# One core, attention and a mixture of experts: the last selection in another order, half of a comparison on GpSimd and ScalarE, the first block of tokens copied alone

## The chip, the cores and the metric

The kernel runs on one NeuronCore of a Trainium2 chip. Its engines work side by side and each takes its own instructions in the order of the program: TensorE (PE, with the weight loads as PEld), VectorE (DVE), ScalarE (ACT), GpSimd (POOL) and SyncE (SP), which issues most DMAs. An instruction waits on semaphores for what other engines owe it, and everything behind it on its engine waits too. The metric is the device time of one execution in microseconds, the median of several.

## The reference

Causal attention for 8 batches, 12 heads, 448 positions and 64 values per head, then a mixture of 8 experts over the 3584 tokens of 768 values. Each token goes to one expert, the one with the largest gate logit; an expert keeps at most 80 tokens, those with the largest gate weight. All other rows of the result are zero.

```python
scores = scale * np.matmul(q, k.transpose(0, 1, 3, 2))
attn = softmax(np.where(mask, -1e9, scores))
x = (attn @ v).transpose(0, 2, 1, 3).reshape(N, D)
logits = x @ w_gate
expert_idx = np.argmax(logits, axis=1)
gate_w = softmax(logits)[np.arange(N), expert_idx]
for e in range(E):
    tok_idx = np.where(expert_idx == e)[0]
    if len(tok_idx) > capacity:
        keep = np.argpartition(-gate_w[tok_idx], capacity)[:capacity]
        tok_idx = tok_idx[keep]
    h = np.maximum(x[tok_idx] @ w1[e], 0.0)
    out[tok_idx] = gate_w[tok_idx, None] * (h @ w2[e])
```

(The softmax is written short here.)

## The kernel before, in words

**Attention.** The batches follow each other. Heads go in pairs; for each pair the scores, the masked softmax, the transposes of the probabilities and the products with v are laid out by hand over eight slots. Queries and keys are split into two float16 parts (GpSimd and VectorE subtract, L387 and L395). The rows that attention gives go to a buffer in memory, xs.

**Selection.** After each batch its tokens are gated, and a table with the 80 best tokens of each expert so far is merged with those of the new batch. `gate` (L623 on) makes the logits, subtracts the largest (gsh, L641), marks the chosen expert (goh, L648 and L659) and makes the weights (ggw, gow). `select_groups` then writes the one-hot rows and the weight, cut into three bfloat16 parts, to mv (L703 to L716). Two transposes (selt, L731) and copies on ScalarE (ex, L734) turn one-hots and weights into rows. From these come rl and lt (L761, L767), which compare the tokens of the batch with the table; cp and ro, the new ranks of the table's tokens (L774, L779); rn and less (L745, L748), which compare the tokens of the batch with each other in four parts; gt, own and rank, their ranks (L813 to L830). `place` (L783) compares ro with the slot numbers and gives rm, one-hot for the table's tokens, in two halves of four experts each; rr (L849) is the same for the new tokens. The products of rm and rr with the table and mv give the new table tn (L859, L862).

For the first seven batches all this lies under the next batch's attention. After the last batch nothing is left to hide it. There the order is written out by hand in the string `TAIL`: every name is a step, issued in this order on all engines. `r0w` to `r7w` turn the eight blocks of attention's rows on TensorE, `r0e` to `r7e` take them to SBUF on the engine that `ROW_ENGINES` names, and divide by the softmax's sums: "v" does it on VectorE, "a" in six multiplications on ScalarE (L605), "p" copies on ScalarE (L607) and scales on GpSimd (L619, step `r0m` to `r7m`); then a DMA to xs follows. `hold` issues a copy of one column on GpSimd (L721) that depends on the gating, so what stands behind it on GpSimd waits for VectorE. "*2" issues two products without use that keep TensorE busy (L1108).

**Experts.** `finish` (L915) makes the indices of the chosen tokens and their weights. `gather` fetches an expert's 80 tokens from xs with an indirect DMA (L1197), which waits for all of the DMAs to xs. `inputs` (L1202) transposes them (xtp) and splits them into float16 parts h and l, or for blocks of weights that are used whole, in float32, copies them as w (xw). Weights are split too: ScalarE casts them to wh (L1180), VectorE makes the remainder wl (L1165). Expert 0 begins with the three blocks of w1 that are used whole, so its first product (hp, L1231) needs xw alone. In this part only TensorE's order is written by hand; on the other engines a scheduler has set it.

Of the kernel before, what the change touches and what calls it, by code (L numbers as in the profile page):

```python
# [7 lines left out]
F32 = mybir.dt.float32  # L8
F32R = mybir.dt.float32r
F16 = mybir.dt.float16  # L10
BF16 = mybir.dt.bfloat16
I32 = mybir.dt.int32
AF = mybir.ActivationFunctionType
ALU = mybir.AluOpType
# [3 lines left out]
P = 128  # L18
# [23 lines left out]

TAIL = """
u ta ya tb yb v0 td yd tc yc v1 vy guard invert last_rows w gp0 wy close piece gp1 gs
r0w r0e r1w lp r1e r1m r2w r2e rest rest r3w r3e lg logit shifted chosen rest rest r4w r4e r5w *2
sums one_hot wsum one_zero wmore columns r0t r0c *2 weight weighted parts hold r1t r1c rl r3m r4m r5e r5m r6w r6e r6m
lt c3w c3l cp c2w r7w r7e r7m ro c2l c1w gt3 *1 c0w c1l gt2 *1 c0l *1 gt1 places *1 earlier gt0 places_more own *3 rank rr tn tab *17
"""
ROW_ENGINES = "vpappppp"


@with_exitstack
def attention_then_moe(
# [12 lines left out]
    nc = tc.nc  # L66
    B, _, NP, S = qT.shape
    N, D = out.shape
    E = wg.shape[2]
# [3 lines left out]
    NT = (S + P - 1) // P  # L73
    NC1 = D // P
    NC2 = F // P
    LAST = S - (NT - 1) * P
    CAP = max(0, min(int(capacity), N))
# [8 lines left out]
    spool = sel_stack.enter_context(tc.tile_pool(name="sel", bufs=2, side="right"))  # L86
    ps_m = ctx.enter_context(tc.tile_pool(name="ps_m", bufs=2, space=PSUM))
# [30 lines left out]
    SL = max(2, min(P, CAP))  # L118
    NSL = (CAP + SL - 1) // SL
# [12 lines left out]
    for r in range(2):  # L132
        t = akeep.tile([P, OFF_L + NT * P], F32, name=f"prob{r}")
# [7 lines left out]
    for r in range(2):  # L141
        t = akeep.tile([P, NT, PH * P], F32, name=f"vt{r}")
# [41 lines left out]
    wmore = [wearly]  # L184
# [37 lines left out]
    lg = keep.tile([P, NT, H * E], F32, name="lg")  # L222
# [468 lines left out]
    def select_groups(bt):  # L691

        b = bt.b
        last = b == B - 1
        sm = lambda name, shape, dt=F32: spool.tile(shape, dt, name=name, tag=name, bufs=1)
# [23 lines left out]
        def hold():  # L719

            nc.gpsimd.tensor_copy(sm("held", [P, 1]), bt.rest[:, 0, 0:1])  # L721

        def expert_rows(i):
            got = []
# [55 lines left out]
                bt.moves.append((table[s][0], ro, sn))  # L780
            return [weights, less, counts, ranks]

        def place(ro, sn, s, rm=None):  # L783

            n = min(SL, CAP - s * SL)
            halves = [(0, E // 2), (E // 2, E)]
            if rm is not None:
                halves.pop(0)
            elif NSL == 1:
                halves.pop()  # L790
            if rm is None:
                rm = spool.tile([SL, E, SL], BF16, name="rm", tag="rm", bufs=1 if NSL == 1 else 2)
            for e0, e1 in halves:
                nc.vector.tensor_tensor(
                    out=rm[0:sn, e0:e1, 0:n], in0=ro[0:sn, e0:e1].unsqueeze(2).to_broadcast([sn, e1 - e0, n]),
                    in1=slots_e[0:sn, s, e0:e1, 0:n], op=ALU.is_equal)
            return rm
# [10 lines left out]
        def later_part(t):  # L808

            if t == NT - 1:  # L810
                bt.gt = ps_m.tile([P, NT, E], F32, name="gt", tag="misc")
            for u in range(t + 1):
                nc.tensor.matmul(bt.gt[:, u, :], bt.less[t][:, u * P:(u + 1) * P], bt.oh3[:, t, 0, :],  # L813
                                 start=(t == NT - 1 and u == 0), stop=(t == u), skip_group_check=True)
# [16 lines left out]
            bt.new = []  # L831

        def places():
            if NSL == 1:
                bt.places = [place(ro, so, 0) for tab, ro, so in bt.moves]

        def places_more():
            if NSL == 1:
                for rm, (tab, ro, so) in zip(bt.places, bt.moves):
                    place(ro, so, 0, rm)  # L840

        def move(s):
# [43 lines left out]
            if not last and NSL == 1:  # L886
# [9 lines left out]
        moves = [f for s in range(NSL) for f in move(s)]  # L896
        steps = {"columns": columns, "parts": parts, "r0t": r0[0], "r0c": r0[1], "r1t": r1[0], "r1c": r1[1],
                 "places": places, "places_more": places_more, "earlier": earlier, "own": own, "rank": rank}
        steps.update({"hold": hold, **{f"gt{t}": lambda t=t: later_part(t) for t in range(NT)}} if last else {"gt": later})
        for t in range(NT):  # L900
            steps[f"c{t}w"], steps[f"c{t}l"] = cmp[NT - 1 - t]
        if tabs:
# [36 lines left out]
    for b in range(B):  # L939
        bt = Batch()  # L940
# [7 lines left out]
    n = len(pairs)  # L948
# [33 lines left out]
    with tc.manual_schedule():  # L982
# [14 lines left out]
            out=nowhere, out_offset=None, in_=w2.rearrange("e p c (g d) -> (e p c g) d", d=DH)[0:N, :],  # L997
# [10 lines left out]
        deferred, parts = [], []  # L1008
        for i, pr in enumerate(pairs):
            bt = pr.bt  # L1010
# [7 lines left out]
            h = i // PH  # L1018
# [12 lines left out]
            for k in range(SLOTS):  # L1031
# [37 lines left out]
        rest = [f for k in sorted(plan) for f in plan.pop(k)]  # L1069
# [66 lines left out]
    ps = ctx.enter_context(tc.tile_pool(name="ps", bufs=2, space=PSUM, reuse_waits="tile"))  # L1136
# [4 lines left out]
    def whole(e, which, c):  # L1141

        if e >= E - 2:
            return e == E - 1 and which == 2 and c >= NC2 - 1
        return c >= NC2 - 2 if which == 2 else c >= (NC1 // 2 if e == 0 else NC1 - 1)

    SW, SX = 32.0, 8.0
# [3 lines left out]
    PER = NC1 if NC1 * SL <= 512 else NC1 // 2  # L1151
# [50 lines left out]
    def inputs(u):  # L1202

        h = ffn.tile([P, NC1, SL], F16, name="xh", tag="xh")
        l = ffn.tile([P, NC1, SL], F16, name="xl", tag="xl")
        nw = sum(whole(u.e, 1, c) for c in range(NC1))
        w = ffn.tile([P, NC1 // 2, SL], F32, name="xw", tag="xw", bufs=1)
        per = NC1 // 2 if u.e == 0 else PER
        for c0 in reversed(range(0, NC1, per)):
            tp = ps_m.tile([P, per, SL], F32, name="xtp", tag="misc", padded_shape=[P, PER, SL])  # L1210
            for c in range(per):
                nc.tensor.transpose(tp[:, c, :], u.xg[:, (c0 + c) * P:(c0 + c + 1) * P], ident[0:SL, 0:SL])
            part = slice(c0, c0 + per)
            if nw and c0 + per == NC1:
                nc.scalar.activation(w[:, NC1 // 2 - nw:], tp[:, per - nw:], AF.Copy, scale=SX * SW)
            nc.scalar.activation(h[:, part], tp, AF.Copy, scale=SX)
            u.xl = nc.vector.scalar_tensor_tensor(out=l[:, part], in0=tp, scalar=SX, in1=h[:, part], op0=ALU.mult,
                                                  op1=ALU.subtract)
        u.x = h, l, w

    def product(u, a, which, x, n, outs, per, blocks=None, side=None):
# [117 lines left out]
    for s in range(NSL):  # L1339
# [4 lines left out]
        for e in range(E):  # L1344
            u = Unit()
# [9 lines left out]
        with tc.manual_schedule(engines={mybir.EngineType.PE}):  # L1355
            for e in range(E + 1):
                if e < E:
                    u = units[e]
# [77 lines left out]
```

## Time and profile before

| | us |
|---|---|
| three runs, median | 467.88 (467.48 to 468.62) |
| the profiled execution | 467.61 |
| its span | 465.7 |
| attention | to about 333 |
| last selection, to the first expert product | to 351.2 |
| experts, to the last product | to about 459 |

A row of the timeline gives the start from the span's beginning, the duration, the engine, the line, the operation, what it writes and reads with its size (partitions x elements), and in brackets how long the engine stood idle before it and what ended that. Rows that begin with a line are groups, with their count, busy time and mean in ns, or with the shortest, middle and longest duration. A window's row gives each engine's busy time, and the granted TensorE clock (PEclk) as a share of full speed.

### The profile page before, as it was taken

The page shows a single profiled execution, that of the slowest core. Times are in us where ns is not written, and L with a number is a line of the kernel's source. Part 1 is how long each engine was busy: PE and PEld are TensorE (multiplying, and loading weights), DVE is VectorE, ACT ScalarE, POOL GpSimd, SP SyncE. Part 2 cuts the span into 40 slices and gives each one's busy share as a digit, 9 for nine tenths or more (in the row PEclk, how much of TensorE's full clock was granted, in tenths as well). Part 3 has the DMA queues.
Part 4 walks back from the last instruction along what each step waited for, and adds up shares of the span by engine and source line. Part 5 has one row for each costly group of instructions (what it writes and reads, how often), then busy time and mean ns, then how long its engine had stood idle before and what let it go on. Part 6 is the DMA issues. An engine that isn't in the chain of part 4 may idle for free.

```text
span 465.7 us, 14169 instructions
## 1 busy us (share of the span) xinstructions
PE 441.2 (95%) x4973; PEld 346.3 (74%) x4973; DVE 414.5 (89%) x1286; ACT 392.3 (84%) x1077; POOL 309.1 (66%) x382
## 2 busy tenths in 40 slices
PE   4998999999999999999999999999989999999994
PEld 1676666866777786677777767776558999999993
DVE  6888889988998999899899989989589999999792
ACT  6997989878988997898889789888587998988791
POOL 7999999988987987898798789760153133310001
PEclk9999999999999999999999999999999999999999
DMA  8658899989769578966957987439948999999931
GB/s 217 182 158 236 230 304 275 271 242 306 206 209 297 171 232 253 270 184 211 298 163 223 279 243 220 161 129 344 410 157 274 397 391 391 398 425 423 423 132 44
DMA packets 42998, 120.84 MB, mean 260 GB/s; under 512 B 6146, under 2 KB 23810, under 8 KB 39472
## 3 DMA queue, kind: packets, MB, share of 16 engines
q1 hardware_dynamic: 41712, 116.21, 76.8%
q0 software_dynamic: 1056, 3.51, 2.4%
q8 instruction: 39, 0.64, 0.6%
q10 hardware_dynamic: 160, 0.23, 0.2%
q14 instruction: 31, 0.25, 0.2%
HBM read 96.36 MB, written 23.99 MB: 258 GB/s over the span
## 4 chain that ended last, share of the span: by engine, by line
PE 75%; DVE 9%; POOL 5%; DMA 4%; issue 3%; ACT 2%; SPq 1%; POOLq 0%; DVEq 0%; ACTq 0%
PE xp L495 15%; PE tp L465 15%; PE sp L423 6%; PE sp L424 5%; PE rt L592 4%; PE hp L1231 3%; PE op L1231 3%; PE op L1239 3%; PE sp L433 3%; PE gp L545 3%; PE hp L1246 3%; PE hp L1245 3%; PE hp L1243 2%; DMA qk<-k_t 2%; DVE wl L1165 2%
## 5 line engine op out<-in xcount | busy, mean ns | idle before, releaser
L448 ACT ACTIVATE prob<-ns,nb 128x128 f32<-128x128 f32 (+3 forms) x336 | 177.1, 529 | 23.0 <-DVE nb L445 20.6
L445 DVE CUSTOM_DVE_ANT_0 ns<-sp,mask 128x384 f32<-128x384 f32 (+2 forms) x288 | 116.2, 413 | 20.2 <-PE sp L424 16.5
L465 PE MATMUL tp<-ident,prob 128*128 128x128 f32 x768 | 118.4, 277 | 1.1 <-ACT prob L448 0.9
L477 ACT COPY PT<-tp 128x512 f32<-128x512 f32 x182 | 104.1, 573 | 17.8 <-PE sp L423 8.4
L395 POOL TENSOR_TENSOR qk<-qk,qk 128x448 f16<-128x448 f32 x92 | 95.8, 1063 | 13.1 <-DVE qk L387 7.4
L465 PEld LDWEIGHTS tp<-ident,prob 128*128 128x128 f32 x768 | 89.8, 142 | 12.1 <-ACT PT L477 2.5
L1165 DVE SCALAR_TENSOR_TENSOR wl<-wraw,wh 128x768 f16<-128x768 f32 (+1 forms) x91 | 92.5, 1081 | 3.2 <-ACT wh L1180 3.2
L495 PE MATMUL xp<-PT,vt 128*64 128x448 f32 (+3 forms) x768 | 91.1, 380 | 0.0
L495 PEld LDWEIGHTS xp<-PT,vt 128*64 128x64 f32 x768 | 53.8, 137 | 42.7 <-issue 22.7
L423 PE MATMUL sp<-qk 128*128 128x384 f16 (+2 forms) x288 | 75.9, 279 | 8.2 <-ACT qk L355 5.2
L1180 ACT ACTIVATE wh<-wraw 128x768 f16<-128x768 f32 (+1 forms) x91 | 79.0, 931 | 3.6 <-PE hp L1246 1.8
L424 PE MATMUL sp<-qk 128*128 128x384 f16 (+2 forms) x288 | 78.3, 278 | 1.3 <-DVE qk L349 0.8
L448 ACT ACTIVATION_READ_ACCUMULATOR prob<-ns,nb 128x1 f32 x336 | 64.0, 190 | 0.0
L1332 POOL DMA_INDIRECT out<-yo,idx x8 | 14.7, 1832 | 70.8 <-ACT yo L1329 66.6
L390 POOL TENSOR_TENSOR qk<-qk,qk 64x448 f16<-64x448 f32 x46 | 54.8, 1190 | 3.4
L391 POOL TENSOR_TENSOR qk<-qk,qk 64x448 f16<-64x448 f32 x46 | 51.0, 1109 | 3.2
L423 PEld LDWEIGHTS <-qk 128*128 128x128 f16 x288 | 28.5, 99 | 17.3 <-issue 8.0
L387 DVE CAST qk<-qk 128x896 f16<-128x896 f32 x46 | 40.4, 879 | 0.1
L384 POOL CAST qk<-qk 64x896 f16<-64x896 f32 x40 | 37.4, 935 | 4.4 <-PE sp L436 3.2
L1246 PEld LDWEIGHTS <-wl 128*128 128x128 f16 x362 | 36.1, 100 | 0.9 <-DVE wl L1165 0.7
L1243 PEld LDWEIGHTS <-wh 128*128 128x128 f16 x362 | 36.4, 101 | 0.0
L1245 PEld LDWEIGHTS <-wh 128*128 128x128 f16 x362 | 36.2, 100 | 0.0
(192 smaller groups left out, 927.7 us busy)
## 6 DMA issues: line engine op xcount, KB each, us to landing
wraw<-w SPq DMA_DIRECT2D x27, 1536.0 KB, 15.7
qk<-k_t SPq DMA_DIRECT2D x92, 224.0 KB, 5.5
out<-mask_l SPq DMA_DIRECT2D x56, 192.0 KB, 4.6
qk<-q_t SPq DMA_DIRECT2D x23, 448.0 KB, 4.2
vt<-v_t SPq DMA_DIRECT2D x24, 384.0 KB, 5.7
xs<-xr SPq DMA_DIRECT2D x42, 192.0 KB, 2.9
wraw<-w SPq DMA_DIRECT2D x24, 256.0 KB, 5.9
vt<-v_t SPq DMA_DIRECT2D x24, 64.0 KB, 5.3
```

What stands on the lines that cost most here:

```text
L390: nc.gpsimd.tensor_tensor(out=qa[hi, i], in0=qf[lo, i], in1=qa[lo, i], op=ALU.subtract)
L391: nc.gpsimd.tensor_tensor(out=qb[lo, i], in0=qf[hi, i], in1=qb[hi, i], op=ALU.subtract)
L395: nc.gpsimd.tensor_tensor(out=k_lo[j][:, i], in0=kf[j][:, i], in1=k_hi[j][:, i], op=ALU.subtract)
L423: nc.tensor.matmul(sp[:, 0:w], qx[:, p, t * P:w], kx[:, p, 0:w], start=True, stop=False)
L424: nc.tensor.matmul(sp[:, 0:w], qx[:, p, t * P:w], lx[:, p, 0:w], start=False, stop=True)
L445: pr.masked = nc.vector.tensor_tensor_reduce(out=ns[:, 0:w], in0=sp[:, 0:w], in1=m, scale=-1.0 / 8.0, scalar=HUGE, op0=ALU.add, op1=ALU.mi ...
L448: nc.scalar.activation(pr.P[:, off:off + w], ns[:, 0:w], AF.Exp, bias=nb, scale=-1.0, accum_out=total)
L465: nc.tensor.transpose(pr.tp[:, i], pr.P[:, off:off + P], ident)
L477: copy(dst, src)
L495: state["pe"] = nc.tensor.matmul(xp[rows, 0:w], st["vt"][:, c, p * P + j * DH:p * P + (j + 1) * DH], pr.PT[:, j, n0:n0 + w], start=(c == 0 ...
L1165: return nc.vector.scalar_tensor_tensor(out=l, in0=src, scalar=SW, in1=h, op0=ALU.mult, op1=ALU.subtract)
L1180: nc.scalar.activation(h, src, AF.Copy, scale=SW)
```

## The change

Four things are different, all of them after attention.

1. `TAIL` is reordered. r2 is no longer scaled on ScalarE but on GpSimd, r7 no longer on GpSimd but on ScalarE (`ROW_ENGINES`); the scalings r2m, r3m and r4m stand further ahead, and the turns r6w and r7w too. The product rl stands ahead of the second transposed block, and the counts of keep-warm products differ.
2. The second half of `place` in the last selection is no longer an `is_equal` on VectorE. `apart` takes the difference of ro and the slot number on GpSimd and squares it; `joined` gives relu(1 - d*d) on ScalarE, which is one where they are equal and zero otherwise.
3. The first half stays on VectorE, where it stood (`places`).
4. `inputs` of expert 0 transposes and copies the first float32 block alone, then the two others, then the float16 blocks. For all experts, blocks that are used whole are no longer also split into h and l.

```diff
-r0w r0e r1w lp r1e r1m r2w r2e rest rest r3w r3e lg logit shifted chosen rest rest r4w r4e r5w *2
-sums one_hot wsum one_zero wmore columns r0t r0c *2 weight weighted parts hold r1t r1c rl r3m r4m r5e r5m r6w r6e r6m
-lt c3w c3l cp c2w r7w r7e r7m ro c2l c1w gt3 *1 c0w c1l gt2 *1 c0l *1 gt1 places *1 earlier gt0 places_more own *3 rank rr tn tab *17
+r0w r0e r1w lp r1e r1m r2w r2e rest rest r2m r3w r3e lg logit shifted chosen rest rest r4w r4e r3m r5w r5e *3
+sums one_hot wsum one_zero wmore columns r6w *2 r0t r0c r7w r6e *1 weight weighted parts r4m hold *1 rl r1t r1c lt *2 c3w r5m r6m c3l cp c2w
+ro places_more c2l c1w r7e moved *2 gt3 *1 c0w c1l gt2 *1 c0l gt1 places *1 earlier gt0 own *5 rank rr tn tab *20
-ROW_ENGINES = "vpappppp"
+ROW_ENGINES = "vppppppa"
...
+            bt.one = sm("one", [P, 1])
+            nc.gpsimd.memset(bt.one, 1.0)
...
+        def apart(ro, so):
+            d = sm("apart", [SL, E // 2, SL], BF16)
+            half = d[0:so, :, 0:CAP]
+            bt.apart.append((half, so))
+            nc.gpsimd.tensor_tensor(out=half, in0=ro[0:so, E // 2:E].unsqueeze(2).to_broadcast([so, E // 2, CAP]),
+                                    in1=slots_e[0:so, 0, E // 2:E, 0:CAP], op=ALU.subtract)
+            nc.gpsimd.tensor_tensor(out=half, in0=half, in1=half, op=ALU.mult)
+            return spool.tile([SL, E, SL], BF16, name="rm", tag="rm", bufs=1)
+
+        def joined():
+            for rm, (half, so) in zip(bt.places, bt.apart):
+                nc.scalar.activation(rm[0:so, E // 2:E, 0:CAP], half, AF.Relu, bias=bt.one[0:so], scale=-1.0)
...
-        per = NC1 // 2 if u.e == 0 else PER
-        for c0 in reversed(range(0, NC1, per)):
-            tp = ps_m.tile([P, per, SL], F32, name="xtp", tag="misc", padded_shape=[P, PER, SL])
+        parts = [(0, NC1)] if u.e else [(NC1 // 2, NC1 // 2 + 1), (NC1 // 2 + 1, NC1), (0, NC1 // 2)]
+        for i, (c0, c1) in enumerate(parts):
...
+            split = [c for c in range(c0, c1) if not whole(u.e, 1, c)]
+            m = len(split)
+            if m < n:
+                nc.scalar.activation(w[:, c0 + m - NC1 // 2:c1 - NC1 // 2], tp[:, m:], AF.Copy, scale=SX * SW)
+            if m:
+                nc.scalar.activation(h[:, c0:c0 + m], tp[:, 0:m], AF.Copy, scale=SX)
```

What this makes of the engines' order is shown at three places; line numbers behind the diff's places are higher in the changed kernel (the cast of weights, L1180, is L1201 there).

ScalarE, from the first row copy of the last selection to the first copies of expert 0's tokens, before (xrl are attention's rows, tab and row the table, wh the cast weights):

```order
L607 COPY xrl<-rt 128x384
L605 ACTIVATE xrl<-rt,sums 128x64 x6
L873 CAST tab_0_678<-tn 80x40
L607 COPY xrl<-rt 64x384
L646 ACTIVATE gex<-gsh 128x32
...
L734 COPY ex<-selt 24x512 x2
L607 COPY xrl<-rt 128x384 x2
L607 COPY xrl<-rt 64x384
L1180 ACTIVATE wh<-wraw 128x1024 x8
L1215 ACTIVATE xw<-xtp 128x240
L1216 ACTIVATE xh<-xtp 128x240 x2
```

The same place in the changed kernel:

```order
L607 COPY xrl<-rt 128x384 x2
L894 CAST tab_0_678<-tn 80x40
L607 COPY xrl<-rt 64x384
L646 ACTIVATE gex<-gsh 128x32
...
L736 COPY ex<-selt 24x512
L605 ACTIVATE xrl<-rt,rql 64x64 x6
L853 ACTIVATE rm<-apart,one 80x320
L1201 ACTIVATE wh<-wraw 128x1024 x8
L1241 ACTIVATE xw<-xtp 128x80
L1241 ACTIVATE xw<-xtp 128x160
L1243 ACTIVATE xh<-xtp 128x240
```

The six multiplications have moved from r2 to r7, the Relu (L853) has come in ahead of the eight casts of weights, and the copy to xw is in two parts.

GpSimd, from the first row scaling to the first gather, before (mv gets the columns of the batch's tokens):

```order
L619 TENSOR_TENSOR xrl<-xrl,sums 128x384
L703 TENSOR_TENSOR mv<-goh,tbase 128x4x8
L705 TENSOR_TENSOR mv<-goh,pnum 128x4x8
L721 COPY held<-grest 128x1
L619 TENSOR_TENSOR xrl<-xrl,rql 64x384
L619 TENSOR_TENSOR xrl<-xrl,sums 128x384 x3
```

And in the changed kernel:

```order
L619 TENSOR_TENSOR xrl<-xrl,sums 128x384 x2
L619 TENSOR_TENSOR xrl<-xrl,rql 64x384
L703 TENSOR_TENSOR mv<-goh,tbase 128x4x8
L705 TENSOR_TENSOR mv<-goh,pnum 128x4x8
L619 TENSOR_TENSOR xrl<-xrl,sums 128x384
L721 COPY held<-grest 128x1
L723 MEMSET one 128x1
L619 TENSOR_TENSOR xrl<-xrl,sums 128x384 x2
L846 TENSOR_TENSOR apart<-ro_6399,slots_e 80x320
L848 TENSOR_TENSOR apart<-apart 80x320
```

Three scalings now stand ahead of "held" where one stood, and the two operations of `apart` follow the last scaling.

VectorE, the last comparisons before the gather, in the changed kernel; before, a second row "rm<-ro" of 80x320 stood between rank and own:

```order
L750 SCALAR_TENSOR_TENSOR less_6324,parts<-rn,ggw,before 128x128
L796 TENSOR_TENSOR rm<-ro_6399,slots_e 80x320
L822 TENSOR_TENSOR parts<-parts,lower_6377 128x4
L823 TENSOR_TENSOR rank<-number_after,parts 128x4
L827 TENSOR_TENSOR own<-gt,goh 128x32
L829 TENSOR_REDUCE larger<-own 128x4
```

One row of VectorE is gone there, and the others stand as before.

More of the change, by code (lines that the diff above doesn't have):

```diff
@@ L781, in table_chunk, with place @@
             return [weights, less, counts, ranks]
-        def place(ro, sn, s, rm=None):
+        def place(ro, sn, s, rm=None, half=1):
             n = min(SL, CAP - s * SL)
@@ L787, in place @@
             if rm is not None:
-                halves.pop(0)
+                halves = halves[half:half + 1]
             elif NSL == 1:
@@ L833, in places @@
         def places():
-            if NSL == 1:
+            if last and NSL == 1:
+                for rm, (tab, ro, so) in zip(bt.places, bt.moves):
+                    place(ro, so, 0, rm, 0)
+            elif NSL == 1:
                 bt.places = [place(ro, so, 0) for tab, ro, so in bt.moves]
+        def apart(ro, so):
[9 more added lines that the diff above has]
+                nc.scalar.activation(rm[0:so, E // 2:E, 0:CAP], half, AF.Relu, bias=bt.one[0:so], scale=-1.0)
         def places_more():
-            if NSL == 1:
+            if last and NSL == 1:
+                bt.apart = []
+                bt.places = [apart(ro, so) for tab, ro, so in bt.moves]
+            elif NSL == 1:
                 for rm, (tab, ro, so) in zip(bt.places, bt.moves):
@@ L898, in select_groups @@
                  "places": places, "places_more": places_more, "earlier": earlier, "own": own, "rank": rank}
-        steps.update({"hold": hold, **{f"gt{t}": lambda t=t: later_part(t) for t in range(NT)}} if last else {"gt": later})
+        steps.update({"hold": hold, "moved": joined if NSL == 1 else lambda: None, **{f"gt{t}": lambda t=t: later_part(t) for t in range(NT)}} if last else {"gt": later})
         for t in range(NT):
@@ L1205, in inputs @@
         l = ffn.tile([P, NC1, SL], F16, name="xl", tag="xl")
-        nw = sum(whole(u.e, 1, c) for c in range(NC1))
         w = ffn.tile([P, NC1 // 2, SL], F32, name="xw", tag="xw", bufs=1)
-        per = NC1 // 2 if u.e == 0 else PER
-        for c0 in reversed(range(0, NC1, per)):
-            tp = ps_m.tile([P, per, SL], F32, name="xtp", tag="misc", padded_shape=[P, PER, SL])
[L1211 to L1218, printed above, removed]
+        parts = [(0, NC1)] if u.e else [(NC1 // 2, NC1 // 2 + 1), (NC1 // 2 + 1, NC1), (0, NC1 // 2)]
+        for i, (c0, c1) in enumerate(parts):
+            n = c1 - c0
+            if i == 0 and len(parts) > 1:
+                tp = ps.tile([P, n, SL], F32, name="xtp", tag="o", padded_shape=[P, PER, SL])
+            else:
+                tp = ps_m.tile([P, n, SL], F32, name="xtp", tag="misc", padded_shape=[P, PER, SL])
+            for c in range(n):
+                nc.tensor.transpose(tp[:, c, :], u.xg[:, (c0 + c) * P:(c0 + c + 1) * P], ident[0:SL, 0:SL])
+            split = [c for c in range(c0, c1) if not whole(u.e, 1, c)]
+            m = len(split)
+            assert split == list(range(c0, c0 + m))
+            if m < n:
+                nc.scalar.activation(w[:, c0 + m - NC1 // 2:c1 - NC1 // 2], tp[:, m:], AF.Copy, scale=SX * SW)
+            if m:
+                nc.scalar.activation(h[:, c0:c0 + m], tp[:, 0:m], AF.Copy, scale=SX)
+                u.xl = nc.vector.scalar_tensor_tensor(out=l[:, c0:c0 + m], in0=tp[:, 0:m], scalar=SX, in1=h[:, c0:c0 + m],
+                                                      op0=ALU.mult, op1=ALU.subtract)
         u.x = h, l, w
```

## Prediction

> **What bounds the kernel now.** I read the page's chain first, then a table of three stretches (the end of the selection, the expert layers, the end).
>
> ```profile
> PE 75%; DVE 9%; POOL 5%; DMA 4%; issue 3%; ACT 2%; SPq 1%; POOLq 0%; DVEq 0%; ACTq 0%
> core 0: us, PE busy (x) PEld busy (x) DVE busy (x) ACT busy (x) POOL busy (x), PEclk, DMA share, GB/s
> 335.00:351.20 16.20, 12.83 (x116) 8.05 (x114) 13.60 (x52) 13.46 (x28) 9.07 (x12) 1.00 0.53 195
> 351.20:455.00 103.80, 103.67 (x1933) 103.52 (x1934) 100.17 (x126) 90.27 (x148) 21.85 (x12) 1.00 0.92 363
> ```
>
> From 351.2 to 455.0 us TensorE is busy 103.67 of 103.80 us: whatever moves the first expert product moves the end by about as much. All of the change that can matter lies in the 16 us before, where TensorE waits. What released that first product stands in the chain of waits in order of time, and ScalarE's timeline shows it whole:
>
> ```profile
> 345.39 0.50 DVE rr L849
> 350.14 0.64 PE L1212 MATMUL xtp<-ident,xg 80*128 80x80 f32 x6 [0.65 <-DMA xg<-xs,idx]
> 342.70 1.05 ACT L1180 ACTIVATE wh<-wraw 128x1024 f16<-128x1024 f32 x1
> 344.13 6.74 ACT L1180 ACTIVATE wh<-wraw 128x1024 f16<-128x1024 f32 x7 [0.38 <-DMA xs<-xrl]
> 350.78 0.34 ACT L1215 ACTIVATE xw<-xtp 128x240 f32<-128x240 f32 x1
> 351.18 0.34 PE L1231 MATMUL hp<-xw,wraw 128*128 128x80 f32 x1 [0.40 <-ACT xw L1215]
> ```
>
> Two paths meet at xw. One is the selection on VectorE, the index, the gather and the transposes of the tokens, whose first bank is ready about half way through its 0.64 us, near 350.5. The other is ScalarE, which takes instructions in order and has eight casts of weights (wh) ahead of xw: they hold it until 350.78. The casts already end last, by 0.2 to 0.3 us. So a selection that finishes sooner buys nothing unless the casts also start sooner.
>
> **The change, step 1: row copies sooner on GpSimd.** Before, GpSimd stands idle while VectorE works out the gating; the copy "held" (L721) keeps the scalings of rows behind it.
>
> ```profile
> 336.02 0.83 POOL L619 TENSOR_TENSOR xrl<-xrl,sums 128x384 f32<-128x384 f32 x1 [2.32 <-ACT xrl L607]
> 338.49 0.26 POOL L703 TENSOR_TENSOR mv<-goh,tbase 128x32 bf16<-128x32 f32 x1 [1.64 <-DVE goh L669]
> 338.72 0.23 POOL L705 TENSOR_TENSOR mv<-goh,pnum 128x32 bf16<-128x32 f32 x1
> 339.84 0.82 POOL L619 TENSOR_TENSOR xrl<-xrl,rql 64x384 f32<-64x384 f32 x1
> 336.11 1.34 ACT L605 ACTIVATE xrl<-rt,sums 128x64 f32<-128x64 f32 x6 [0.17 <-PE rt L592]
> 337.38 0.49 ACT L607 COPY xrl<-rt 64x384 f32<-64x384 f32 x1
> 337.24 0.19 DVE L641 TENSOR_TENSOR gsh<-logit,gmx 128x32 f32<-128x32 f32 x1
> 337.47 0.19 DVE L648 SCALAR_TENSOR_TENSOR goh<-gsh,dec 128x32 f32<-128x32 f32 x1
> 339.10 0.18 DVE L713 CAST mv<-gow 128x32 bf16<-128x32 f32 x1
> 339.64 0.19 DVE L716 TENSOR_TENSOR mv<-grest,mv 128x32 bf16<-128x32 f32 x1
> ```
>
> After, the scalings of r2 and r3 follow r1 at once and r4 stands ahead of "held". What GpSimd does beside VectorE's small operations is to be seen in earlier batches (all executions of L648, then one of them with its neighbour on GpSimd, then two casts' spread):
>
> ```profile
> L648 DVE SCALAR_TENSOR_TENSOR goh<-gsh,dec x8: 191/679/851, 65.7 to 337.5; 128x32 f32<-128x32 f32 x8
> 65.44 1.04 POOL L390 TENSOR_TENSOR qk<-qk,qk 64x448 f16<-64x448 f32 x1
> 65.68 0.85 DVE L648 SCALAR_TENSOR_TENSOR goh<-gsh,dec 128x32 f32<-128x32 f32 x1
> L387 DVE CAST qk<-qk x46: 602/623/2770, 12.5 to 302.3; 128x896 f16<-128x896 f32 x46
> ```
>
> L648 takes 0.19 us alone, and in this very stretch, but 0.68 to 0.85 beside a GpSimd operation: it ends 0.05 us after GpSimd does (66.53 against 66.48). I take that price. r2 runs from 336.85 to 337.67 (0.82, as r1's row), so gsh ends at 337.72 in place of 337.43; r3 runs to 338.49, so goh ends at 338.54 in place of 337.66: **+0.88 us**. r3's copy on ScalarE (L607, 337.38 before) is early enough, since r2 now takes one such copy of 0.49 us there, not the six multiplications of 1.34. With all of it 0.88 later, L705 ends at 339.83 and r4 holds GpSimd until 340.65. The cast L713 would start at 339.98; like L387, whose spread shows that casts wait too, it then ends at 340.70 in place of 339.28: **+1.42 in all**. Were casts free, only the operation with two inputs behind it would wait, and the sum here would be 1.20; that is the lower bound. I take 1.42, as L387 is a cast of the same two types.
>
> The Trainium skill, page "SBUF — State Buffer", section on its two separate sides, says that VectorE and GpSimd share one pair of SBUF ports under an exclusive lock: an operation of VectorE with two SBUF inputs or in a two-port mode waits for the whole GpSimd instruction. By that rule step 1 costs 1.42; if the engines only shared bandwidth, nearly nothing (rival B). The rows of L648 side with the rule.
>
> **Step 2: rl ahead of the second transposed block.**
>
> ```profile
> 338.72 0.40 PE L731 MATMUL selt<-identb,oh 128*128 128x128 bf16 x4
> 339.15 0.57 ACT L734 COPY ex<-selt 24x512 bf16<-24x512 bf16 x1 [0.50 <-PE selt L731]
> 339.98 0.38 PE L731 MATMUL selt<-identb,mv 128*128 128x128 bf16 x4 [0.49 <-POOL held L721]
> 340.20 0.31 PE L761 MATMUL rl<-row,ex 128*128 128x80 bf16 x4
> 340.55 0.30 DVE L767 TENSOR_SCALAR_CACHE_REDUCE lt<-rl,ggw 128x80 bf16<-128x80 f32 x1 [0.71 <-PE rl L761]
> 341.03 0.38 PE L745 MATMUL rn<-ex 128*128 128x512 bf16 x1 [0.17 <-ACT ex L734]
> 341.44 0.75 DVE L748 SCALAR_TENSOR_TENSOR less<-rn,ggw,before 128x512 bf16<-128x512 f32 x1
> 342.12 0.22 DVE L779 TENSOR_SCALAR ro<-cp,pnum 80x8 f16<-80x8 f32 x1
> ```
>
> VectorE idles 0.71 us for rl, which stood behind the second selt; now rl comes first. But the first "less" needs rn, and rn needs the second selt, which needs mv: 341.44 is 1.61 us after mv ends (339.83), by way of selt, ex and rn, and none of that gets shorter. Lt has its 0.9 us of slack filled either way. So the swap is worth nothing, and "less" and ro follow mv: ro ends at 342.34 + 1.42 = 343.76. The extra keep-warm products stand where TensorE waits; before the gather they now number 20 at 0.2 us, 0.1 us at most ever in the way.
>
> **Step 3: half of the comparison on GpSimd and ScalarE.**
>
> ```profile
> 343.47 0.08 DVE L748 DVE_READ_ACCUMULATOR less<-rn,ggw,before 128x1 f32 x1
> 343.00 0.82 POOL L619 TENSOR_TENSOR xrl<-xrl,rql 64x384 f32<-64x384 f32 x1
> 343.47 0.70 DVE L794 TENSOR_TENSOR rm<-ro,slots_e 80x320 bf16<-80x320 f16 x1
> 344.36 0.48 DVE L794 TENSOR_TENSOR rm<-ro,slots_e 80x320 bf16<-80x320 f16 x1
> L395 POOL TENSOR_TENSOR qk<-qk,qk 128x448 f16<-128x448 f32 x92 | 95.8, 1063 | 13.1 <-DVE qk L387 7.4 <-POOL qk L391 3.7
> L1263 ACT ACTIVATE hh<-hp 128x320 f16<-128x320 f32 x9 | 3.7, 425 | 0.0
> ```
>
> VectorE loses the second L794, 0.40 us of its path. In its place GpSimd runs two operations of 80x320 on 16-bit data, which no row shows. L619 (384 columns, 0.82) and L703 (32 columns, 0.26) put 320 columns on a line at 0.72; L395 (1.06 for 448, writing 16 bits) gives 0.76 by share and 1.06 as an upper end. I take 0.75 each. Beginning 0.10 after ro: 343.86 to 344.61, and 344.65 to 345.40. The Relu on ScalarE is like L1263 (0.43 us, the next one 0.35 after its start): it starts at 345.48, and **the eight casts now stand behind it**, so they start at 345.83, not 342.70. Seven of them took ScalarE from 344.13 to 350.78, 0.95 each; eight take 7.60. ScalarE reaches xw at **353.43**.
>
> VectorE's side has meanwhile come to: last "less" 343.55 + 1.42 = 344.97, rm held by GpSimd to 345.74 (L794 ends 0.34 after it: 344.17 against 343.82), rr 0.82 later at 346.56, which is 1.17 later than before; tokens at 350.14 + 1.17 = 351.31, transposed by 351.95. The casts end 1.5 us after that, so they set the time.
>
> **Step 4: the first float32 block alone.**
>
> ```profile
> 357.27 0.24 ACT L1215 ACTIVATE xw<-xtp 128x80 f32<-128x80 f32 x1 [2.70 <-PE xtp L1212]
> ```
>
> The first copy takes 0.24, as this one of 80 columns does, rather than 0.34 us: hp starts at 353.43 + 0.24 + 0.05 = **353.72, against 351.18: +2.54**. The narrower copies of the other experts (480 to 400 columns, about 0.08 us each on VectorE and ScalarE) are off the path while TensorE is full; with the few tenths that TensorE waited in the expert layers I give back 0.2. Bounds of this: 0 to 0.7.
>
> **Sum.** The profiled execution took 467.61 us, its span 465.7 us, the median of the three runs is 467.88; the 0.27 between them are less than the bounds and are not added. 467.61 + 2.54 - 0.2 = 469.95, say **469.9 us**. From the unknown costs: step 1 lower by 0.22, step 3 higher by 0.62 (two at 1.06), give-back up to 0.7: 469.2 to 470.6.
>
> **Rivals.** *B, no waiting for GpSimd.* Mv stays at 339.83. Rl waits for the first copy to ex (339.72) and for TensorE's row turn and keep-warm ahead of it, an estimated 339.98 in place of 340.20, so the second selt, behind it, comes 0.16 late and ro ends at 342.50. The casts still stand behind GpSimd and Relu: 2.07 us later at 344.57, xw at 352.17, hp at 352.44, +1.26, with the give-back 468.7. For it: "own" and other reads of PSUM never show waits; against it: L648. *C, not slower: the expert layers take the delay up.* Weight loads and VectorE (100.17 of 103.80) are nearly as full as TensorE; if one of them set the end, hp could start up to 2.5 us later for nothing, and the result is 467.6. It decides from the point at which TensorE has gaps worth 1.4 us in that stretch; its row leaves 0.13. *D, worse:* GpSimd's operations near 1.06, and its three row scalings each waiting on VectorE in turn (another 0.5): 471.0. *E, the change does what it says:* only if the casts began by 342.6 could the gather (0.40 sooner) set the time, hp 350.6, 467.0; ro itself ends at 342.34 before, so two GpSimd operations do not fit.
>
> **How the numbers follow.** The forecast (casts late by steps 1 and 3) 0.66, B 0.18, C 0.06, D 0.08, E 0.02. The range that leaves out only C and E and takes in the bounds is 468.3 to 471.3. A measurement of this kernel tells 0.3%, 1.4 us, from no change. The forecast and D are above that, a sixth of B too; the rest of B and most of C are within; so slower 0.75, same 0.22, and 0.03 for faster, out of C and E, for a saving that I don't see.
>
> **What would show it.** Right: wh starts near 345.8, directly behind Relu; xw waits for ScalarE, not for xtp; L641 and L648 at 0.4 to 1.0 us; TensorE idle 1 to 2 us between xtp and hp. Step 1 wrong: L648 at 0.19. Step 3 wrong: GpSimd's two operations under 0.5 us. All of it is wrong if xw starts directly behind the transposes.

## The result, and the profile after

| | before | after |
|---|---|---|
| median | 467.81 us | 474.69 us (473.87 to 476.37) |
| ratio after / before | | 1.0149 (95% interval 1.0136 to 1.0163) |
| the profiled execution | 467.61 us | 475.72 us |
| its span | 465.7 us | 473.5 us |
| mean granted TensorE clock | 0.999 | 0.981 |

The change makes the kernel 6.9 us slower. Slower was forecast, by 2.1 us; 474.69 lies above the upper end of the forecast range, 471.3.

The page of the profile after shows in one row where to look. PEclk is the granted clock in 40 slices of 11.8 us; the chain's share of TensorE has grown from 75% to 84%.

```profile
PEclk9999999999999999999999999999995999999998
...
PE 84%; DVE 7%; ACT 5%; issue 2%; DMA 1%; POOL 0%; POOLq 0%; SPq 0%; DVEq 0%; ACTq 0%
```

The table of stretches of the changed kernel places it: the selection, the 13.6 us behind the first expert product, and the rest.

```profile
core 0: us, PE busy (x) PEld busy (x) DVE busy (x) ACT busy (x) POOL busy (x), PEclk, DMA share, GB/s
335.00:353.65 18.65, 14.92 (x128) 9.06 (x126) 14.59 (x51) 13.92 (x29) 11.61 (x16) 1.00 0.46 154
353.65:367.22 13.57, 13.57 (x91) 13.57 (x92) 7.56 (x9) 4.55 (x9) 1.22 (x2) 0.50 0.85 295
367.22:459.00 91.78, 91.78 (x1737) 91.76 (x1735) 88.41 (x112) 82.25 (x133) 11.63 (x9) 1.00 0.92 364
```

TensorE is "busy" in the whole of the middle stretch, at a granted clock of 0.50: 91 products, where the 13.57 us behind the first expert product before hold 254:

```profile
351.18:364.75 13.57, 13.57 (x254) 13.57 (x254) 13.14 (x17) 10.78 (x18) 2.58 (x3) 1.00 0.97 318
```

Busy time alone doesn't show it; the column PEclk does.

ScalarE's and TensorE's timelines, after (two fences, one for each engine):

```profile
334.71 0.53 ACT L550 COPY gs<-gp 96x448 f32<-96x448 f32 x1 [2.01 <-PE gp L545]
345.34 0.56 ACT L853 ACTIVATE rm<-apart,one 80x320 bf16<-80x320 bf16 x1 [1.79 <-POOL apart L848]
345.81 7.67 ACT L1201 ACTIVATE wh<-wraw 128x1024 f16<-128x1024 f32 x8
353.38 0.40 ACT L1241 ACTIVATE xw<-xtp 128x80 f32<-128x80 f32 x2
```

```profile
351.22 0.63 PE L1236 MATMUL xtp<-ident,xg 80*128 80x80 f32 x6
353.65 10.53 PE L1258 MATMUL hp<-xw,wraw 128*128 128x80 f32 x48 [1.79 <-ACT xw L1241]
363.97 1.01 PE L1236 MATMUL xtp<-ident,xg 80*128 80x80 f32 x6
```

The forecast chain is there, row by row: the Relu, eight casts behind it, xw at 353.38 (353.43 forecast), the first expert product at 353.65 (353.72). What is new is the length of that product's row: the same 48 product passes that took 5.58 us now take 10.53. Before, the copy of the gate's products, gs, and that row stood so (again one fence for each engine):

```profile
334.62 0.53 ACT L550 COPY gs<-gp 96x448 f32<-96x448 f32 x1 [2.02 <-PE gp L545]
```

```profile
351.18 5.58 PE L1231 MATMUL hp<-xw,wraw 128*128 128x80 f32 x48 [0.40 <-ACT xw L1215]
```

Attention does not end at the same moment in every execution, so from here on times of the selection are counted from the start of gs (334.71 after, 334.62 before), and those of the expert layers from the first expert product. With the starts of xtp rows in TensorE's timeline as marks:

| stretch | before | after | difference |
|---|---|---|---|
| gs to the first expert product | 16.56 | 18.94 | +2.38 |
| from there to the transposes for expert 1 | 5.42 | 10.32 | +4.90 |
| to those for expert 2 | 11.64 | 13.16 | +1.52 |
| to those for expert 7 | 67.62 | 67.33 | -0.29 |
| to TensorE's last product | 23.87 | 23.07 | -0.80 |

They add up to 7.71 us of the 7.8 by which the span grew. The first row was forecast (2.54). The next two, 6.42 us, hold the stretch at half clock. The last two are a gain, of 1.1 us.

### The profile page after: what moved, and what is told of

It reads as the page before. It is cut to its first block, busy times and chain, and to the rows that moved or that the text cites. A ratio compares the mean times of both kernels' runs of the same rounds, so it can differ in the third digit from the quotient of the medians.

```text
span 473.5 us, 14192 instructions
## 1 busy us (share of the span) xinstructions
PE 448.1 (95%) x4984; PEld 353.2 (75%) x4984; DVE 415.2 (88%) x1284; ACT 393.1 (83%) x1078; POOL 301.2 (64%) x385
## 4 chain that ended last, share of the span: by engine, by line
PE 84%; DVE 7%; ACT 5%; issue 2%; DMA 1%; POOL 0%; POOLq 0%; SPq 0%; DVEq 0%; ACTq 0%
PE xp L495 17%; PE tp L465 16%; PE sp L423 7%; PE sp L424 6%; PE hp L1258 4%; PE rt L592 4%; PE op L1266 4%; PE op L1258 3%; PE gp L545 3%; PE sp L433 3%; PE hp L1272 3%; PE hp L1273 3%; PE hp L1270 3%; DVE ns L445 2%; PE op L1268 2%
## 5 line engine op out<-in xcount | busy, mean ns | idle before, releaser
L395 POOL TENSOR_TENSOR qk<-qk,qk 128x448 f16<-128x448 f32 x92 | 97.1, 1077 | 13.6 <-DVE qk L387 8.0
L1201 ACT ACTIVATE wh<-wraw 128x768 f16<-128x768 f32 (+1 forms) x91 | 79.1, 930 | 4.8 <-PE hp L1273 2.1
L1359 POOL DMA_INDIRECT out<-yo,idx x8 | 9.4, 1175 | 74.3 <-ACT yo L1356 70.3
L387 DVE CAST qk<-qk 128x896 f16<-128x896 f32 x46 | 40.7, 885 | 1.3 <-DMA qk<-k_t 1.3
L1270 PEld LDWEIGHTS <-wh 128*128 128x128 f16 x362 | 37.0, 102 | 0.0
L1272 PEld LDWEIGHTS <-wh 128*128 128x128 f16 x362 | 36.8, 102 | 0.0
```

The costliest lines, as they stand in the source:

```text
L395: nc.gpsimd.tensor_tensor(out=k_lo[j][:, i], in0=kf[j][:, i], in1=k_hi[j][:, i], op=ALU.subtract)
L1201: nc.scalar.activation(h, src, AF.Copy, scale=SW)
L1270: nc.tensor.matmul(o, wh[:, ws], ah[:, c, :], start=(x == 0 and i % per == 0), stop=False, skip_group_check=True)
```

## The experiments

The kernel before ran beside each group of four: 468.16, 467.26 and 467.44 us. What happened at TensorE's clock, and whether 2.4 us were the casts' alone, had to be separated. The first four kernels: fill the idle time; shorten ScalarE's queue; take the comparison back; and delay xw in the kernel before, without any of the change.

**fill.**

```diff
                         inputs(u)
+                        wp = ps.tile([P, S], F32, name="wq", tag="o")
+                        for _ in range(9):
+                            nc.tensor.matmul(wp, identb, before[:, 0:S], start=True, stop=True)
```

> The changed kernel, with nine more keep-warm products (0.19 us each, 1.7 us) between the first transposes of the tokens and the first expert product, where TensorE stood idle for 1.79 us. They write a bank of their own. Theory (the delay of 2.5 us is that of the casts; the other 4 to 5 us come from the granted clock, which fell to 0.50 because TensorE stood idle): clock 1.00 throughout, first expert product still at about 353.6 us, time 467.8 + 2.5 - 0.2 = 470.1 us. Rival (the clock falls for another reason, or the expert layers lose the time otherwise): 474.7 us as before.

473.34 us, ratio 1.0115 (1.0083 to 1.0147). TensorE's timeline of fill:

```profile
350.43 0.63 PE L1236 MATMUL xtp<-ident,xg 80*128 80x80 f32 x6
350.90 1.87 PE L1398 MATMUL wq<-before,identb 128*128 128x448 bf16 x9
353.05 5.58 PE L1258 MATMUL hp<-xw,wraw 128*128 128x80 f32 x48 [0.28 <-ACT xw L1241]
...
367.32 0.20 PE L1273 MATMUL hp<-xh,wl 128*128 128x80 f16 x1 [1.39 <-issue]
```

The first expert product comes as late as in the changed kernel (18.93 us behind gs), and its row is 5.58 us long again: with the idle time filled the clock stays up there. But two costs came in. In expert 1 TensorE stands for 1.39 us in which it waited for nothing that the profile shows, and 1.5 us later the clock falls, for 3.41 us. So the theory held for the idle time that was filled, and the time of the whole could not show it.

**four_casts.**

```diff
-                        units[1].order, more = split_pieces(n1)
                         for nx in units[1:AHEAD]:
                             gather(nx)
...
                         inputs(u)
+                        units[1].order, more = split_pieces(n1)
```

> The changed kernel, with expert 1's weights cast behind expert 0's tokens: four casts of weights stand ahead of xw on ScalarE, not eight. Theory (xw waits for casts that begin late): ScalarE is through with them at 345.8 + 4 x 0.95 = 349.6 us, so xw follows the first transposes at about 351.45, the first expert product comes at about 351.8, TensorE has no long idle time, clock 1.00, and the time is 467.8 + 0.6 = 468.4 us. Rival (the selection is late by itself, with the casts only beside it): xw no earlier than 352.5 and the time over 470 us.

470.34 us, ratio 1.0052 (1.0033 to 1.0071). ScalarE's timeline of this kernel:

```profile
345.12 3.88 ACT L1201 ACTIVATE wh<-wraw 128x1024 f16<-128x1024 f32 x4
350.88 0.43 ACT L1241 ACTIVATE xw<-xtp 128x80 f32<-128x80 f32 x2 [1.88 <-PE xtp L1236]
```

ScalarE now waits 1.88 us for the tokens instead of the tokens for it, and the first expert product comes 17.16 us behind gs (17.1 expected). So the casts alone held xw, and the selection by itself is 0.6 us late. The clock did not fall. The time is 2 us over what was expected: from the first expert product to the last it takes 110.98 us in place of 108.55. TensorE stands for 0.94 us in expert 1, again without a releaser, and waits for VectorE's wl in the last expert, which takes 25.53 us in place of 23.87.

**whole_rm.** `places` and `places_more` compare both halves on VectorE, as in the kernel before; `apart` and `joined` are not called.

> The changed kernel without its second and third part: both halves of the comparison are made on VectorE again, as before; the order of the row copies, rl first and the first block alone stay. Theory: no Relu stands ahead of the casts, so they begin behind the last scaling of rows, at about 343.5, and end at 351.2; rr comes 0.3 us later than in the changed kernel, at 346.8; the first expert product at 351.8 to 352.1, no clock drop, time 468.3 to 468.7 us. Rival (the row copies that hold VectorE back cost most of it): over 470 us.

467.55 us, ratio 0.9987 (0.9973 to 1.0001): without the second and third part of the change, and so without a Relu ahead of the casts, the time is that of the kernel before. The first expert product stands at 17.17 us, and the clock did not fall, although TensorE's timeline has this stall, shorter than that of fill:

```profile
366.28 1.01 PE L1252 MATMUL hp<-xw,wraw 128*128 128x80 f32 x8 [1.02 <-issue]
```

**more_casts.** The kernel before, and ahead of xw (with xw and the copies behind it placed behind the last of these):

```diff
+                        spare = wsplit.tile([P, F], F16, name="spare")
+                        for _ in range(2):
+                            with tc.issue_after(batches[-1].raised.ins):
+                                spares.append(nc.scalar.activation(spare, wload[0][:, 0, :], AF.Copy, scale=SW))
```

> The kernel before, with three more casts ahead of xw on ScalarE, two of them without use (1024 columns, 0.95 us each) and one of 768 columns that came later; nothing else is changed, GpSimd and the selection least of all. Theory (a late xw alone does it: TensorE idle, then half the clock): xw 2.6 us later, the first expert product at 353.8 us after an idle time of 3 us, clock 0.50 for 10 to 14 us, time 467.8 + 2.6 + 5 = 475.4 us. Rival (the drop needs something else of the change): clock 1.00 and 470.3 us.

475.08 us, ratio 1.0151 (1.0114 to 1.0189): as slow as the changed kernel, with none of its edits. TensorE's timeline:

```profile
353.07 10.53 PE L1235 MATMUL hp<-xw,wraw 128*128 128x80 f32 x48 [2.53 <-ACT xw L1218]
```

A late xw alone, by way of an idle TensorE, makes both the delay and the row of 10.53 us. The rival (470.3) is out.

The next four look for the idle time that it takes, for the stall, and for the price of the row copies.

**one_more_cast.** As more_casts, with `range(1)`.

> The kernel before with a single cast without use (1024 columns, 0.95 us) ahead of xw. TensorE is then idle for 0.4 + 0.95 = 1.35 us behind the first transposes. Theory: xw 0.95 us later; whether the clock falls tells from how long an idle time it does so (0.94 to 1.02 us did not do it, 1.39 and more did). Without the fall 468.8 us, with it 473.5 us. Rival (any late xw costs as much as three casts did, 7 us): 474 us or more.

473.57 us, ratio 1.0113 (1.0036 to 1.0189). The first expert product came 0.45 us later than in the kernel before (17.01 us behind gs), after an idle time of 0.90, not 1.35: ScalarE did not wait for a DMA among its casts as it had done in the profile before (0.38). And yet the clock fell, for 13.65 us. So the idle time behind the transposes is not the measure by itself. Leaving out the last one, behind the last expert product, the stretches at 0.50 are 3.41 us long in every kernel here, or two or four times that (6.83, 13.65), and so the 3.41 us ahead of each fall are the stretch to look at. Each row below gives such a stretch, with TensorE's busy time, the granted clock and the DMA. First the changed kernel:

```profile
350.16:353.57 3.41, 1.61 (x12) 1.00 0.60 139
```

more_casts:

```profile
348.41:351.82 3.41, 1.49 (x11) 1.00 0.29 82
```

one_more_cast:

```profile
348.51:351.92 3.41, 1.91 (x17) 1.00 0.43 105
```

fill:

```profile
365.41:368.82 3.41, 2.02 (x29) 1.00 0.94 370
```

whole_rm_short (below):

```profile
339.76:343.17 3.41, 1.83 (x21) 1.00 0.46 166
```

The kernel before, where the clock held: its least busy 3.41 us near the first expert product, and in the gating:

```profile
348.00:351.41 3.41, 2.36 (x16) 1.00 0.30 82
...
336.70:340.11 3.41, 2.25 (x20) 1.00 0.85 345
```

TensorE was busy for 1.49 to 2.02 us of 3.41 ahead of these falls. From the gating to the first expert product the kernel before never goes under 2.25, and the change took 0.75 away at the last place (2.36 to 1.61). But busy time is no sharp measure. In rl_first (below) the clock fell after 2.42 us (first row), and in the attention of the kernel before it held through a stretch of 1.99 and behind it (second row):

```profile
341.50:344.91 3.41, 2.42 (x24) 1.00 0.63 211
```

```profile
44.44:47.85 3.41, 1.99 (x17) 1.00 0.59 210
```

So no bound follows from these traces, and what is counted stays open. The time at full clock between two falls is a whole number of such stretches too (in the changed kernel 102.40 us, 30 of them, from 367.22 to 469.62): the stretches of a trace lie on one grid. Where the grid lies against the work differs from trace to trace (the falls come 18.86 us behind gs in the changed kernel, 17.44 in more_casts, 18.00 in one_more_cast), so the same idle time may fall into one stretch or be shared by two; no run tried that by itself.

**whole_rm_short.** whole_rm with the eleven counts of keep-warm products 1, 1, 0, 0, 1, 0, 1, 1, 0, 3, 20 in place of 3, 2, 1, 1, 2, 2, 1, 1, 1, 5, 20.

> The kernel whole_rm with 28 keep-warm products in place of 39, as many as before the change. Theory (the stall of 1.02 us in expert 1 goes with the length of TensorE's program): no such stall, and otherwise as whole_rm (first expert product 17.2 us behind gs): 467.8 to 466.6 us, 0.9 below whole_rm where nothing else takes the gain. Rival (the stall belongs to the inputs copied in another order): the stall stays, 467.5 us.

468.73 us, ratio 1.0022 (0.9997 to 1.0047). The stall in expert 1 is gone, with 11 products fewer in TensorE's program (107.46 us from the first expert product to the last, 108.60 in whole_rm). But without the keep-warm products in the selection the clock fell there (at 343.17, for 6.83 us), the last 20 of them ran at half speed past the tokens' arrival, and the first expert product came at 18.59 us. The products that look like filling each carry the clock.

**fill_short.** The changed kernel with 26 keep-warm products (1, 1, 0, 0, 1, 0, 1, 0, 0, 2, 20) and two float32 ones, `nc.tensor.matmul(wp, ident, wload[0][:, 0, 0:S])`, where fill had nine.

> The changed kernel with two float32 products without use between the first transposes and the first expert product (an estimated 1.5 us, in the place where TensorE stood idle for 1.79 us), and 13 of the 39 keep-warm products of the last selection left out, so that TensorE's program is about as long as before. Theory (the clock falls because TensorE stands idle; the fill's stall of 1.39 us in the expert layers comes from where TensorE's code is fetched, and goes with the length of its program): the first expert product 18.9 us behind the gate's copy gs, as in the changed kernel, clock 1.00, no stall in expert 1, 108.6 us from the first expert product to TensorE's last, as before; time 467.8 + 2.4 = 470.2 us. Rival (the stall belongs to the change itself): again 1 to 1.5 us of stall 12 to 14 us behind the first expert product, 472 to 473 us.

471.89 us, ratio 1.0096 (1.0072 to 1.0119). No stall in expert 1; but the clock fell in the selection here too, at 343.47 for 6.83 us, and the first expert product came at 19.88 us. So it gives no price for the change's own fall.

**rl_first.** whole_rm_short with the scalings r2m, r3m and r4m back behind hold (in the changed kernel four scalings stand ahead of it, with r1m, where one did before):

```diff
-... r2w r2e rest rest r2m r3w r3e lg ... r4w r4e r3m r5w r5e *1
+... r2w r2e rest rest r3w r3e lg ... r4w r4e r5w r5e *1
-... weight weighted parts r4m hold rl ...
+... weight weighted parts hold r2m r3m r4m rl ...
```

> The kernel whole_rm_short with r2m, r3m and r4m behind hold again: no GpSimd scalings of rows beside VectorE's gating. Theory (VectorE's small operations wait for GpSimd): goh takes 0.19 us instead of 0.75, the end of the gating (mv) comes 1.3 us sooner, at 5.0 us behind gs, ro at 7.5; the tokens are transposed 1.0 us sooner unless GpSimd's later scalings hold up the gather, and the first expert product then waits for ScalarE's casts alone, at 16.5 to 16.9 us behind gs. Time 0 to 0.5 us below whole_rm_short. Rival (no such wait): the gating as long as in the changed kernel (mv at 6.3 us).

469.71 us, ratio 1.0048 (1.0008 to 1.0087); here too the clock fell, in the selection (344.91, for 3.41 us), and the ten executions lie between 466.99 (the one profiled) and 472.90 us, so the time says little. What bears on step 1 stands in VectorE's timeline, first of whole_rm_short, then of rl_first:

```profile
336.72 0.44 DVE L641 TENSOR_TENSOR gsh<-logit,gmx 128x32 f32<-128x32 f32 x1
337.19 0.75 DVE L648 SCALAR_TENSOR_TENSOR goh<-gsh,dec 128x32 f32<-128x32 f32 x1
339.36 0.67 DVE L713 CAST mv<-gow 128x32 bf16<-128x32 f32 x1
```

```profile
336.72 0.19 DVE L641 TENSOR_TENSOR gsh<-logit,gmx 128x32 f32<-128x32 f32 x1
336.94 0.19 DVE L648 SCALAR_TENSOR_TENSOR goh<-gsh,dec 128x32 f32<-128x32 f32 x1
338.56 0.18 DVE L713 CAST mv<-gow 128x32 bf16<-128x32 f32 x1
```

The same three operations, with and without a scaling on GpSimd beside them; the last part of mv starts at 6.31 us behind gs in the one and at 5.01 in the other. That is 1.30 us for step 1 (1.42 forecast), the cast included. And rl ahead of the second transposed block brought nothing: ro starts at 7.49 us, 7.51 in the kernel before.

The last four: the idle time filled without a longer program, and what of the change is of use.

**fill_f32.** The changed kernel, the last 20 keep-warm products made as 5 in float32, and two such ahead of the first expert product.

> The changed kernel with the last 20 keep-warm products made as 5 float32 products (an estimated 0.75 us each, as long in all), and two more such products between the first transposes and the first expert product. TensorE's program gets shorter by that, and the other keep-warm products of the selection, whose absence let the clock fall in fill_short, are all there. Theory (2.4 us from the casts, the rest from the clock): clock 1.00 from the selection on, first expert product 18.9 us behind gs, no long stall in expert 1, TensorE's last product 108 to 109 us behind the first; 467.5 + 2.4 = 470 us. Rival (the rest comes from the expert layers, not from the clock): 472 us or more although the clock stays at 1.00.

471.02 us, ratio 1.0073 (1.0058 to 1.0087). TensorE's timeline:

```profile
353.00 1.71 PE L1402 MATMUL wq<-wraw,ident 128*128 128x448 f32 x4
354.92 5.58 PE L1262 MATMUL hp<-xw,wraw 128*128 128x80 f32 x48 [0.21 <-ACT xw L1245]
```

The first expert product is at 18.94 us, exactly as late as in the changed kernel; the clock stays at 1.00 from the selection to the last product, nothing stalls in expert 1, and from the first product to the last it takes 109.12 us, not 113.88. Filling 1.8 us of idle time wins 4.8 us there. The time is still 1 us more than expected. One cost that the changed kernel does not have is in the profile: the weight loads wait six times for wl in the last expert, 1.4 us in all.

**before_inputs.** The kernel before with the new `inputs` alone.

> The kernel before with the change's fourth part alone (expert 0's first block copied alone, whole blocks not split as well). Theory: the casts still hold xw until 16.1 us behind gs, the narrower copy saves 0.1 us, hp at 16.45; and the expert layers are 0 to 1 us shorter by the narrower copies of the other experts (whole_rm_short: 107.5 us from the first expert product to the last, against 108.6): 466.3 to 467.3 us where before stands at 467.4. Rival (this part costs something): over 467.8 us.

465.90 us, ratio 0.9963 (0.9950 to 0.9976), **faster than the kernel before and than the changed one**. ScalarE's timeline:

```profile
342.35 7.68 ACT L1180 ACTIVATE wh<-wraw 128x1024 f16<-128x1024 f32 x8
350.13 0.43 ACT L1220 ACTIVATE xw<-xtp 128x80 f32<-128x80 f32 x2
```

The first expert product comes at 16.15 us (16.56 before): about 0.3 because the eight casts ran without the 0.38 us for a DMA, and 0.1 from the narrower copy. The first of the two is not clearly the edit's: one_more_cast did not have that wait either. The expert layers take 107.61 us (108.55), of which 0.81 is in the last expert: there the weight loads no longer wait for wl.

**inputs_v.** before_inputs with `ROW_ENGINES = "vpappppv"` and `r7w` ahead of `weight`, `r7e` behind `parts`.

> The kernel before_inputs with the last block of rows, r7, turned earlier and scaled by VectorE in the 0.71 us in which it waits for rl, in place of ScalarE's copy (0.49 us, the last thing ahead of the casts) and GpSimd's last scaling (0.82 us). Theory (xw waits for the casts, and the tokens are there 0.3 us sooner): casts begin 0.4 us sooner, at 7.7 us behind gs, and the first expert product comes 0.3 to 0.5 us sooner than in before_inputs, at 16.0; 0.4 us below before_inputs. Rival (VectorE's selection gets longer by the scaling): ro after 7.51 us, no gain or up to 0.6 us slower.

465.79 us, ratio 0.9963 (0.9950 to 0.9976). Ro stays at 7.51 us, so the scaling fits into VectorE's wait; the first expert product comes 0.2 us sooner (15.94). The time is that of before_inputs.

**square.** inputs_v with four casts ahead of xw as in four_casts, ro in float32, and in place of both comparisons:

```diff
+                    for e in range(E):
+                        nc.scalar.activation(d[0:so, e, 0:CAP], slots_e[0:so, 0, e, 0:CAP], AF.Square, bias=ro[0:so, e:e + 1], scale=-1.0)
+                    nc.scalar.activation(rm[0:so, :, 0:CAP], d[0:so, :, 0:CAP], AF.Relu, bias=one[0:so], scale=-1.0)
```

> The kernel inputs_v with the whole comparison of ro taken off VectorE and off GpSimd: ScalarE makes (ro - slot)^2 in eight instructions of 80x80 (about 0.2 us each) and relu(1 - d*d) in one of 80x640 (about 0.75 us), and only four casts of weights, not eight, stand between these and xw. Theory: VectorE's path loses its two comparisons (1.0 us), rr comes at 9.8 us behind gs in place of 10.78, the gather 0.8 to 1.0 us sooner, and the first expert product at 15.5 to 15.8 us in place of 16.56: 0.8 us below before_inputs, unless the later casts cost it again in the expert layers as in four_casts (1.2 us). Rival (the gather waits for the writes of the rows, not for the index): first expert product at 16.0 us or later.

468.89 us, ratio 1.0033 (1.0020 to 1.0046). Rr came at 10.27 us (10.56 in inputs_v), not at 9.8, the gather later than in inputs_v by 0.06 us, and the first expert product at 15.99. What ended last here was rm: ScalarE took 2.12 us for the eight squares and 0.83 for the Relu, and the product for the new table waited for that:

```profile
345.54 0.48 PE L870 MATMUL tn<-tab,rm 80*80 80x5 bf16 x8 [0.50 <-ACT rm L843]
```

So ScalarE, used in this way, does not shorten the path either, and the casts moved behind xw cost as in four_casts: the expert layers take 110.66 us, 3.2 more than in inputs_v. The waits of its weight loads:

```profile
PEld L1263 <- DVE wl L1176: 1.7, 6, 0.5
```

## Why the prediction was wrong

**Step 1 was right.** 1.42 forecast; in the changed kernel the last part of mv starts 1.29 us later (6.32 against 5.03 us behind gs), and rl_first takes it away with the scalings. The cast L713 waits as well (0.68 us, 0.18 in rl_first), so the lower bound of 1.20 is out. (The prediction took that from L387 as a cast of the same two types, which it is not: it writes float16, L713 bfloat16.) Rival B (no waiting) falls, and the Trainium skill's rule ("SBUF — State Buffer", its section on two separate sides: VectorE waits out GpSimd's whole instruction) agrees with these rows, at 0.44 and 0.75 us for what takes 0.19.

**Step 2 was right.** Rl sooner is worth nothing; ro follows mv.

**Step 3 was right.** GpSimd's two operations took 0.72 each (0.75), the Relu 0.56, the casts 7.67 (7.60), and xw waited for them: four_casts and whole_rm each take 1.8 us of the delay away, by different ways.

**Step 4** gave 0.1 us as forecast. But the part does more in the expert layers than the 0.2 us of the sum and its bound of 0.7: 0.94 us in before_inputs, most of it waits for wl in the last expert. This term was too small, and its error works against the one that follows.

**The step that failed is the sum's end: "+2.54 - 0.2".** It carried the delay of the first expert product over to the end of the kernel at an unchanged speed of TensorE, as the prediction's first reading has it: whatever moves that product moves the end by about as much. The prediction named the cause itself, among the signs that would show it right, "TensorE idle 1 to 2 us between xtp and hp", and gave it no price. That idle time came (1.79 us), left TensorE busy for 1.61 us of 3.41, and the clock fell to 0.50 for 13.65 us: 6.42 us more. With the delay, 2.38 where 2.54 was forecast, and less the gain of 1.09, that is the 7.71 us. fill and fill_f32 take this fall away with the delay left in; more_casts makes both without the change. None of the rivals was this one; D (471.0) was later for other reasons. Rival C, that the expert layers take a delay up, falls: in fill_f32 they begin 2.38 us late and take 109.12 us, no less than the 108.55 before. (Two sums in the prediction are off by 0.02, without consequence: rival B's first product comes out at 352.46, and its parts for slower add up to 0.77.)

The Trainium skill names a mechanism ("TensorE: Matmul & The Clock Gate", Part 1, what's actually happening): a gate that looks at windows of about 3.4 us. The 3.41 us of these traces agree. By the table there the clock halves after an idle window, and 1.8 us of idle time would then be harmless; here falls followed windows in which TensorE was busy 1.91 and 2.02 us (one_more_cast, fill), so the measurement differs. By its other row the full clock returns after one busy window, which does not fit either: TensorE was busy throughout from 353.65, and the clock came back only at 367.22, at the end of a window that held 16-bit products for its last 2.45 us. Whether the float32 products ahead of them count for less is an inference from that order of things, and was not tried alone.

Open as well: why TensorE stood for 0.94 to 1.39 us in expert 1 in whole_rm, four_casts and fill. It goes when TensorE's program is shorter (by 11 keep-warm products in whole_rm_short). The profile's instruction queue moves one block within 2 us ahead of each stall, but it does so at that place in the kernel before too (between 362 and 364 us), which does not stall. So the fetch of code is a guess that nothing here shows; the changed kernel, at half clock at that place, does not have the stall.

## What to carry to other kernels

Where a wait makes TensorE idle, price two things: the wait, and what the clock does after it. Take the granted clock and TensorE's busy time in stretches of 3.41 us around the place, and compare them with the stretches of the same traces in which the clock held and in which it fell. That gives a warning and no bound: a delay of 0.45 us cost 6 us in one_more_cast, after a stretch that was busy for 1.91 us, while one of 1.99 us passed without a fall elsewhere.

An engine that takes its work in order pays for a new instruction at the front of its queue with everything behind it: one Relu of 0.56 us, waiting for GpSimd and through it for the late ro, moved eight casts by 3 us. Ask what is queued behind it, and who waits for the last of that.

## What was not expected of the hardware

- The granted clock falls after 3.41 us in which TensorE was still busy for 1.5 to 2.0 us, and once after 2.42, but held after 1.99 in the kernel before; it then stays at 0.50 for one, two or four such stretches.
- At half clock the 48 float32 product passes took 10.53 us, busy all the time, and the clock did not rise in them; at full clock (5.58 us) it did not fall in them either.
- Keep-warm products left out of the selection (8 of 19 kept, in whole_rm_short) let the clock fall there, and the 20 left ran into the next work.
